# Delta-rule recurrence into a soft mixture of experts: the last step's outputs by features first, one softmax phase for the last two steps, second weights in whole rows, output columns 208 and 176, norms with fewer VectorE steps

## The chip, the cores and the metric

The kernel runs on one core of a Trainium2 chip. The metric is the device time of one execution in microseconds (us). All data are float32. Engines are named as in the profile: PE (TensorE products; PEld its weight loads), DVE (VectorE), ACT (ScalarE), POOL (GpSimd), and SP, whose queue issues most transfers.

## The reference

The first half is a delta-rule attention, the second a soft mixture of experts over its output:

```python
# q, k, v: (B, H, S, D) = (4, 8, 768, 48); beta: (B, H, S)
k_n = k / (np.linalg.norm(k, axis=-1, keepdims=True) + 1e-06)
for t in range(S):
    y[:, :, t] = q_t @ state                       # per batch and head, state is 48 x 48
    v_old = state^T k_t
    state = state + beta_t * outer(k_t, v_t - v_old)
x = y.transpose(0, 2, 1, 3).reshape(3072, 384)     # tokens x features
logits = x @ phi                                   # 32 slots = 8 experts x 4
d = softmax of logits over the tokens;  slot_input = d.T @ x
slot_out[e] = relu(slot_input[e] @ w1[e]) @ w2[e]  # w1: 384 x 1024, w2: 1024 x 384
c = softmax of logits over the slots;   out = c @ slot_out
```

(The three lines in the loop are shortened from products over all batches and heads.) Sums in the two softmaxes get 1e-9 added.

## The kernel before, in words

The sequence is cut into 12 steps n of 64 tokens, for all 32 pairs of batch and head at once; two steps make a pair g. Within a step the recurrence is solved in closed form: a Gram matrix of the keys is inverted as a triangular system, and the step's update of the state is a product with that inverse. The stages and their lines:

- **Preparing a step.** q, k and v are fetched by SP's queue (L497, L512). Keys and queries are turned (L563, copied by L574), their Gram matrices are formed (L589) and copied with masks: keys by ACT (L620, and L618 on DVE for n = 1) into a tile Gk of 16 rows of three 32-blocks, queries by L639 to L649. L675 adds two of the blocks into Gd, on POOL, for n = 1 on DVE.
- **Inverting a pair** (`invert`). DVE spreads Gd (L727); the squared norms stand on the diagonal. DVE takes a maximum with 1e-30 (L740), ACT a logarithm and an exponential (L744, L745), POOL and DVE one correction step and the weights (L750 to L759), DVE copies the weights to the diagonal of a second tile (L761) and scales (L767). Fifteen columns are solved (L777, L781). The norms are turned (L784) and put in place by POOL (L787). L799 to L818 turn the result back.
- **Joining** (`join`), for each step: small blocks are combined to 32 and 64 by products (L854, L872, L906, L917) and copies between them (L845 to L927).
- **The step** (`step`). v is scaled (L944); key products with the state (L959) are subtracted (L966); W(n) is the product with the inverse (L979, `chain[n]` in the code), copied as U (L1003); L989 adds the queries' part of the output, L1017 and L1026 update the state, L1041 the rest of the output, copied as Y by L1052. In the last step Y is formed and copied in two halves.
- **Routing and phases.** Y is turned (L1077, L1084), the logits are formed (L1102) and kept in Lt (L1108). A phase gathers the softmax over tokens for several steps with a running maximum (reduction L1150, exponential L1162, transposes L1170 and their copy L1172, slot products L1180, sums L1186). Phases cover steps (0 to 3), (4 to 7), (8 to 10), (11).
- **The rest.** L1279 turns the sums into slot inputs, copied by L1281. `first` multiplies them with the first weights (L1304, relu, transposes L1320), `second` with the second (L1339), in two parts of 192 output columns; L1348 to L1351 finish the slot outputs. `combine` forms the softmax over slots for a pair of steps (transposes L1120 and L1135, DVE L1124 to L1133, ACT L1127 and L1137), and waits for L1279. L1361 multiplies it with the slot outputs, for each group of 256 tokens and each batch; L1363 copies, L1365 stores, 24 stores in all.
- **Weights.** The first weights are 48 transfers of 256 KB (L1244); the second 32 of 384 KB (L1254), each four rows of one expert by 192 columns (runs of 768 bytes); the first 16 serve the first part of columns.

The order on each engine is not that of the code. A class `Plan` takes every operation with its engine, inputs, outputs and an assumed duration, and lists them by longest remaining path with a key; keys are moved by a table in the code (SHIFT), and some constants (SLACK, WKEEP, W2KEEP) steer how late or early work and transfers are placed. It also places buffers in one SBUF tile of 52,900 columns and in eight PSUM banks. Each engine then runs its instructions in that order. A product with no use (L480) keeps PE busy where the plan sees a hole at the start and the end.

## Time and profile before

| what | value |
|---|---|
| median of three runs | 284.46 us (282.22 to 285.74) |
| the profiled execution, its own time | 285.92 us |
| its span in the profile | 283.9 us |
| mean granted clock of TensorE | 0.984 |
| busy PE / DVE / ACT / POOL | 253.4 / 203.6 / 164.7 / 99.0 us |
| starts of W(0), W(8), W(11) | 45.66, 184.74, 227.06 us |
| first expert product (L1304) | 240.60 us |
| first, last store issued (L1365); last landing | 262.8, 280.3; 282.6 us |

Times within the profile are counted from the start of the span, and 2.0 us of the execution's own time lie outside it. A busy share is an average over stages: PE is nearly full in the last step and the expert products, and less so before. An engine's idle time matters only where a wait ends last.

### The profile page before, as it was taken

The page shows a single profiled execution, that of the slowest core. Times are in us where ns is not written, and L with a number is a line of the kernel's source. Part 1 is how long each engine was busy: PE and PEld are TensorE (multiplying, and loading weights), DVE is VectorE, ACT ScalarE, POOL GpSimd, SP SyncE. Part 2 cuts the span into 40 slices and gives each one's busy share as a digit, 9 for nine tenths or more (in the row PEclk, how much of TensorE's full clock was granted, in tenths as well). Part 3 has the DMA queues.
Part 4 walks back from the last instruction along what each step waited for, and adds up shares of the span by engine and source line. Part 5 has one row for each costly group of instructions (what it writes and reads, how often), then busy time and mean ns, then how long its engine had stood idle before and what let it go on. Part 6 is the DMA issues. An engine that isn't in the chain of part 4 may idle for free.

```text
span 283.9 us, 13766 instructions
## 1 busy us (share of the span) xinstructions
PE 253.4 (89%) x6038; PEld 211.2 (74%) x6038; DVE 203.6 (72%) x445; ACT 164.7 (58%) x350; POOL 99.0 (35%) x212
## 2 busy tenths in 40 slices
PE   8999998999987989797998998869997999999970
PEld 4777688898876978696986997768886896367860
DVE  2789988989688696789888796869971646941340
ACT  5556498678654698566778479671673452240330
POOL 8933476527730087404474027610330100000000
PEclk9999999999999999999999999989999999999995
DMA  8999982929436390066580994596997889999966
GB/s 99 142 137 145 137 90 41 135 43 139 59 50 68 68 106 3 2 82 93 99 75 2 125 236 97 163 228 218 330 373 265 246 249 322 328 301 329 289 216 223
DMA packets 105834, 45.11 MB, mean 159 GB/s; under 512 B 77008, under 2 KB 99568, under 8 KB 105776
## 3 DMA queue, kind: packets, MB, share of 16 engines
q1 hardware_dynamic: 105600, 44.05, 74.3%
q8 instruction: 47, 0.77, 1.2%
q10 hardware_dynamic: 48, 0.10, 0.3%
q0 software_dynamic: 128, 0.10, 0.2%
q14 instruction: 11, 0.09, 0.1%
HBM read 39.52 MB, written 4.72 MB: 156 GB/s over the span
## 4 chain that ended last, share of the span: by engine, by line
PE 65%; ACT 9%; DMA 7%; issue 6%; DVE 5%; SPq 3%; POOL 1%; ACTq 0%; DVEq 0%; POOLq 0%
DMA sb<-in_k_dram 7%; PE pb L589 6%; PE pb L563 6%; PE pb L989 5%; PE pb L959 5%; PE pb L979 5%; PE pb L480 4%; PE pb L872 4%; PE pb L1339 4%; PE pb L1304 4%; PE pb L1017 4%; PE pb L1041 4%; PE pb L854 3%; PE pb L917 2%; PE pb L1102 2%
## 5 line engine op out<-in xcount | busy, mean ns | idle before, releaser
L574 ACT ACTIVATE sb<-pb 128x1024 f32<-128x1024 f32 x23 | 23.5, 1025 | 17.5 <-PE pb L563 17.4
L620 ACT ACTIVATE sb<-pb,sb 128x256 f32<-128x256 f32 (+1 forms) x47 | 25.6, 574 | 7.1 <-PE pb L589 5.3
L777 DVE TENSOR_TENSOR sb<-sb 128x30 f32<-128x30 f32 (+7 forms) x90 | 27.0, 300 | 2.7
L589 PE MATMUL pb<-sb 48*64 48x64 f32 (+1 forms) x1024 | 26.3, 247 | 2.4 <-ACT sb L574 1.1
L589 PEld LDWEIGHTS pb<-sb 48*64 48x64 f32 x1024 | 22.3, 134 | 6.1 <-ACT sb L574 2.2
L563 PE MATMUL pb<-sb 128*128 128x128 f32 x192 | 25.6, 277 | 1.1 <-DMA sb<-in_k_dram 1.1
L781 DVE TENSOR_TENSOR sb<-sb 128x30 f32<-128x30 f32 (+7 forms) x90 | 23.7, 264 | 3.1
L675 POOL TENSOR_TENSOR sb<-sb 128x512 f32<-128x512 f32 x11 | 14.2, 1289 | 32.8 <-ACT sb L620 28.5
L480 PE MATMUL pb<-sb 128*128 128x512 f32 (+3 forms) x72 | 23.6, 456 | 1.1 <-DVE sb L449 1.1
L563 PEld LDWEIGHTS pb<-sb 128*128 128x128 f32 x192 | 20.9, 141 | 3.0 <-issue 1.4
L895 POOL COPY sb<-sb 32x128 f32<-32x128 f32 x48 | 13.7, 285 | 26.6 <-DVE sb L878 21.7
L1003 ACT COPY sb<-pb 64x768 f32<-64x768 f32 (+1 forms) x24 | 18.4, 765 | 6.1 <-PE pb L979 5.7
L1026 DVE TENSOR_TENSOR sb<-sb,pb 48x768 f32<-48x768 f32 x20 | 19.0, 952 | 3.7 <-PE pb L1017 3.3
L480 PEld LDWEIGHTS pb<-sb 128*128 128x128 f32 x72 | 13.0, 201 | 10.0 <-issue 7.8
L649 POOL TENSOR_SCALAR_AFFINE_SELECT sb<-sb 64x512 f32<-64x512 f32 x24 | 16.2, 676 | 11.1 <-ACT sb L645 6.9
L1041 PE MATMUL pb<-sb 128*64 128x96 f32 x384 | 18.6, 248 | 1.5 <-issue 1.5
L989 PE MATMUL pb<-sb 128*64 128x96 f32 x352 | 18.7, 260 | 0.0
L895 ACT COPY sb<-sb 32x128 f32<-32x128 f32 x48 | 14.2, 295 | 7.3 <-DVE sb L878 5.0
L1052 ACT ACTIVATE sb<-pb 128x768 f32<-128x768 f32 x11 | 8.9, 811 | 16.3 <-PE pb L1041 16.2
L1041 PEld LDWEIGHTS pb<-sb 128*64 128x64 f32 x384 | 16.6, 137 | 2.2 <-issue 1.9
L1017 PE MATMUL pb<-sb 128*48 128x96 f32 x352 | 16.9, 248 | 1.4 <-ACT sb L645 0.7
L884 DVE STREAM_TRANSPOSE sb<-sb 64x512 f32<-64x512 f32 x24 | 16.9, 705 | 0.6
(157 smaller groups left out, 544.9 us busy)
## 6 DMA issues: line engine op xcount, KB each, us to landing
sb<-in_moe_w_dram SPq DMA_DIRECT2D x48, 256.0 KB, 4.7
sb<-in_moe_w_dram SPq DMA_DIRECT2D x32, 384.0 KB, 6.6
sb<-in_k_dram SPq DMA_DIRECT2D x24, 192.0 KB, 5.5
sb<-in_v_dram SPq DMA_DIRECT2D x48, 96.0 KB, 4.4
sb<-in_q_dram SPq DMA_DIRECT2D x24, 192.0 KB, 6.1
out_dram<-sb SPq DMA_DIRECT2D x24, 192.0 KB, 2.5
sb<-in_beta_dram ACTq DMA_DIRECT2D x1, 96.0 KB, 4.9
sb<-in_moe_phi_dram POOLq DMA_DIRECT2D x2, 32.0 KB, 6.0
```

What stands on the lines that cost most here:

```text
L480: pl.filler = lambda b, w: mm(A(b)[:, 0, 0:w].rearrange("p (a f) -> p a f", f=min(w, P)), A(cone), A(cone)[:, 0:min(w, P)].unsqueeze(1).br ...
L563: nc.tensor.transpose(o[:, 128 * j:128 * j + 128], A(src)[:, 128 * j:128 * j + 128], ident())
L574: nc.scalar.activation(o, x, ACT.Copy)
L589: mm(A(ps)[ha(c ^ (j // 4)), i, w * (j - j0):w * (j - j0) + w], kq(n)[hd(i), j, c, 0:C], kq(n)[hd(i), j, c, lo:hi])
L620: nc.scalar.activation(o, i_, ACT.Copy, scale=m)
L777: V.tensor_tensor(p, blk(tt, j, j + 1, 0, m).broadcast_to(sh), blk(lb, j, j + 1, j + 1, 16).rearrange("p x a i -> p x i a").broadcast_to(s ...
L781: V.tensor_tensor(t, t, p, op=ALU.subtract)
L895: (nc.scalar.copy if by_act else nc.gpsimd.tensor_copy)(o[q:q + 32, :, c, i], zx()[64 * c + 32:64 * c + 64, y, i].rearrange("p (j t) -> p ...
L989: mm(ypart(j)[:, :, c], kq(n)[:, j, c, C:2 * C], S0()[:, j, c], start=b % 2 == 0 and c == 0)
L1017: mm(A(pS)[hd(i), j // 4, a:a + 2 * D], A(Kb[n])[:, 128 * j + 64 * i:128 * j + 64 * i + D], U0()[:, j // 4, i, j % 4])
L1026: nc.vector.tensor_tensor(o, o, x, op=ALU.add)
L1041: mm(ypart(j)[:, i], A(AT[n])[:, C * xi(i, j):C * xi(i, j) + C], U0()[:, j // 4, i, j % 4], start=n == 0 and b % 2 == 0 and i == 0)
```

## The change

- The table SHIFT, the constants SLACK, WKEEP and W2KEEP, and several assumed durations are replaced, so the order on every engine is planned anew.
- Norms: the logarithm gets 1e-30 as its bias and reads the diagonal directly, the weights are written to the second tile's diagonal by POOL, so L740 and L761 go; the layout of Gk and Gd is by j first, so L787 goes. Two reciprocals and the turning of the norms stay on DVE.
- Key copies are cut by block (in all 9 of 512 elements and 51 of 256 on ACT, instead of 22 and 25). For n = 1, 2 and 3 the sum into Gd is formed by DVE straight from PSUM (`pack`).
- Last step: the outputs are formed with features on partitions (32 + 32 products of 64 columns), the logits come from that form with a second copy of phi (cphl, four small transfers), and Y is turned back by eight transposes.
- Phases cover (0 to 3), (4 to 7), (8, 9), (10, 11); the last reads its logits from PSUM.
- `combine` no longer waits for L1279; in the new order five of six run among the steps.
- Second weights: 32 transfers of 384 KB, each two whole rows of 384 columns (3 KB runs), all used by both parts of columns; the parts are 208 and 176 columns wide.
- The output products of four batches become one operation, in which successive products use other groups of 32 rows.

```diff
-SLACK = 4.53
+SLACK = 6.8594
...
-    111: -55.2, 112: 3.5, 113: 0.7, 114: 0.6, 115: 0.2, 116: -32.3, 117: -43.4, 118: -124.6,
-    119: -58.4, 120: -98.2, 121: -59.1, 122: -57.4, 123: -156.3, 124: 3.3, 125: -131.3,
-    126: -45.2, 127: 29.5, 128: 181.8, 129: -184.9, 130: 170, 131: -144.2, 132: 56.4, 133: -23.8,
...
@@ -67,7 +70,7 @@
...
     def t_act(c):
-        return 0.17 + 0.00071 * c
+        return 0.23 + 0.0007 * c
...
     LAT, TLD = 2.3, 3.0
-    W1AT, W2AT, W2KEEP = 6, 10, 8741
+    W1AT, W2AT, W2KEEP = 6, 10, 4494.80
...
+        src2 = moe_phi.rearrange("(m i c d) s -> i c d m s", m=2, i=2, c=2)
+        for i in H2:
+            for c in H2:
+                def go2(i=i, c=c):
+                    nc.sync.dma_start(out=A(cphl)[hd(i)].rearrange("p (m c s) -> p c m s", m=2, c=2)[:, c], in_=src2[i, c])
+                pl.op("DMA", 0.3, go2, w=[(cphl, (i, c))], lat=LAT, after=after, key=50)
...
-        def ev(ys, i, lower):
+        def ev(i, b):
             def go():
...
+                x = A(ps).rearrange("p i (j f) -> p j i f", f=w)[:, :, :, 32 * (b > 0):32 * (b > 0) + 32]
+                o, m = Gb(n, b)[:, j0:j0 + nj], M1() if b == 1 else M0()
...
-                ev(H2, i, 1)
+            for b in (0, 1, 2):
+                ev(i, b)
     APART = 4
+    PACKS = (1, 2, 3)
+    def Gt(n):
+        return A(Gd[n // 2]).rearrange("p (t s j i) -> p s j i t", s=2, t=32, i=2)[:, n % 2]
+    def pack(n, j0, nj, ps, w):
+        if n in PACKS:
+            for i in H2:
+                def go(i=i):
+                    x = A(ps)[:, i].rearrange("p (j f) -> p j f", f=w)[:, :, 32:C]
+                    return nc.vector.scalar_tensor_tensor(
+                        Gt(n)[:, j0:j0 + nj, i], x, M1(), Gb(n, 0)[:, j0:j0 + nj, i], op0=ALU.mult, op1=ALU.add)
+                pl.op("DVE", t_dvp(32 * nj), go,
+                      r=[(ps, i), cm0] + [(Gk[n], (0, j0, y)) for y in (None, i)], w=[(Gd[n // 2], (n % 2, j0, i))])
...
                 ps = pl.buf(2, psum=True)
                 gram(n, 0, 2 * C, j0, 4, ps)
                 keys(n, j0, 4, ps, 2 * C)
+                pack(n, j0, 4, ps, 2 * C)
                 queries(n, j0, 4, ps, 2 * C)
-        def pack():
...
-        pl.op("DVE" if n == 1 else "POOL", 0.90 if n == 1 else 1.35, pack, r=[Gk[n]], w=[(Gd[n // 2], n % 2)], port=True)
+        if n not in PACKS:
+            pl.op("POOL", 1.35, lambda: nc.gpsimd.tensor_tensor(Gt(n), Gb(n, 0), Gb(n, 1), op=ALU.add),
+                  r=[(Gk[n], (x, 0, None)) for x in H2] + [(Gk[n], (x, 4, None)) for x in H2], w=[(Gd[n // 2], n % 2)], port=True)
         return og if n < 2 else None
     def prep_q(n):
...
-        ssq, nrm, rn, gm = [pl.buf(32 * G) for _ in range(4)]
+        nrm, rn, gm = [pl.buf(32 * G) for _ in range(3)]
...
-        pl.op("DVE", W_, lambda: V.tensor_scalar(sv(ssq), sv(ssq0) if head else dg(lb), 1e-30, None, op0=ALU.max),
-              r=[ssq0 if head else lb], w=[ssq], key=-25 if head else 0)
+        ssq = ssq0 if head else lb
+        sq = lambda: sv(ssq0) if head else dg(lb)
         def root():
-            nc.scalar.activation(A(nrm), A(ssq), ACT.Ln)
+            nc.scalar.activation(sv(nrm), sq(), ACT.Ln, bias=A(cm0)[:, 7:8])
             nc.scalar.activation(A(nrm), A(nrm), ACT.Exp, scale=0.5)
-        pl.op("ACT", 0.44, root, r=[ssq], w=[nrm])
...
         def norm():
-            G_.tensor_tensor(A(rn), A(rn), A(ssq), op=ALU.mult)
+            G_.tensor_tensor(sv(rn), sv(rn), sq(), op=ALU.mult)
...
-            G_.tensor_tensor(A(gm), A(gm), A(cbb)[:, 32 * gs[0]:32 * gs[0] + 32 * G], op=ALU.mult)
+            G_.tensor_tensor(dg(tt), sv(gm), sv2(cbb), op=ALU.mult)
...
-        pl.op("POOL", 0.57, weight, r=[rn, (cbb, min(gs[0], 1))], w=[gm], port=True)
-        pl.op("DVE", W_, lambda: V.tensor_copy(dg(tt), sv(gm)), r=[gm], w=[tt])
+        pl.op("POOL", 0.57, weight, r=[rn, (cbb, min(gs[0], 1))], w=[gm, tt], port=True)
...
-        nTc = pl.buf(32 * G)
-        pl.op("DVE", 0.14, lambda: V.transpose(A(nTc), A(nrm)), r=[nrm], w=[nTc])
-        def place():
-            nc.gpsimd.tensor_copy(A(nT).rearrange("p (s j i) -> p s i j", s=4 * G, i=2),
-                                  A(nTc).rearrange("p (s i j) -> p s i j", s=4 * G, i=2))
-        pl.op("POOL", 0.2, place, r=[nTc], w=[nT], port=True)
+        pl.op("DVE", 0.14, lambda: V.transpose(A(nT), A(nrm)), r=[nrm], w=[nT])
...
-            pl.op("PE", **t_pe(16, 0.085, 96.0), fn=qs, r=[(KQ[n], 1), (KQ[n], 3), cS], w=[pY],
-                        after=[chain[n]])
-        U0 = lambda: A(cU).rearrange("p (y i j f) -> p y i j f", y=2, i=2, j=4)
...
+            def qst():
+                for j in range(8):
+                    for c in H2:
+                        for i in H2:
+                            a = D * (2 * (2 * j + c) + i)
+                            mm(A(pY)[ha(i), c, C * j:C * j + C], A(cS)[hd(i), a:a + C], kq(n)[hd(i), j, c, C:2 * C],
+                               start=j == 0)
+            if last:
+                pl.op("PE", **t_pe(32, 0.04, 24.0), fn=qst, r=[(KQ[n], 1), (KQ[n], 3), cS], w=[pY])
+            else:
+                pl.op("PE", **t_pe(16, 0.085, 96.0), fn=qs, r=[(KQ[n], 1), (KQ[n], 3), cS], w=[pY],
+                      after=[chain[n]])
...
-        parts = [(None, range(B))] if n < N - 1 else [(o, range(2 * o, 2 * o + 2)) for o in H2]
         Y = Yb[n] = pl.buf(16 * D)
-        for o, bs in parts:
-            def au(bs=bs):
-                for b in bs:
+        if last:
...
+            def aut():
+                for j in range(8):
                     for i in H2:
-                        for j in (2 * b, 2 * b + 1):
-                            mm(ypart(j)[:, i], A(AT[n])[:, C * xi(i, j):C * xi(i, j) + C],
-                               U0()[:, j // 4, i, j % 4],
...
-            oau[n] = pl.op("PE", **t_pe(4 * len(bs), 0.079, 96.0), fn=au,
-                           r=[(b, (y, c)) for b in (AT[n], cU) for y in (H2 if o is None else (o,)) for c in H2],
-                           w=[(pY, o)])
...
...
+                        for c in H2:
+                            a = D * (2 * (8 * (j // 4) + 4 * i + j % 4) + c)
+                            mm(A(pY)[ha(i), c, C * j:C * j + C], A(cU)[ha(c), a:a + C],
+                               A(AT[n])[ha(c), C * xi(i, j):C * xi(i, j) + C], start=False)
+            pl.op("PE", **t_pe(32, 0.0275, 24.0), fn=aut, r=[AT[n], cU], w=[pY])
+            for c in H2:
+                pl.op("DVE" if c else "ACT", t_dvp(512) if c else t_act(512) - 0.03, lambda c=c: (
+                    nc.vector.tensor_copy if c else nc.scalar.copy)(A(YT)[:, 512 * c:512 * c + 512], A(pY)[:, c]),
+                    r=[(pY, c)], w=[(YT, c)])
+            ps = pl.buf(2, psum=True)
+            for o in H2:
+                def back(o=o):
+                    for b in (0, 1):
+                        for c in H2:
+                            x = A(ps)[:, o, 256 * b:256 * b + 256].rearrange("p (i c f) -> p c i f", i=2, c=2)[:, c]
+                            a = 512 * c + 128 * (2 * o + b)
+                            nc.tensor.transpose(x, A(YT)[:, a:a + 128], ident())
+                pl.op("PE", **t_tr(4), fn=back, r=[YT, cident], w=[(ps, o)], key=5)
+                def yev(o=o):
...
+            return
...
-            pl.op("PE", **t_tr(len(qs6)), fn=yt, r=[(Y, o), cident], w=[(ps, o)])
...
-        pL = pl.buf(1, psum=True)
-        w = C * ns
-        parts = [(None, range(B))] if n < N - 1 else [(o, range(2 * o, 2 * o + 2)) for o in H2]
-        for o_, bs in parts:
-            def lg(bs=bs):
...
-            pl.op("PE", **t_pe(4 * len(bs), 0.0297 * ns, 32.0 * ns), fn=lg,
-                  r=[(YT, None if o_ is None else 2 + o_), cphi], w=[(pL, o_)])
...
+        pL = pLb[n] = pLb[n - 1] if n == N - 1 else pl.buf(1, psum=True)
+        w, z0 = C * ns, C if n == N - 1 else 0
+        def lg():
+            if n == N - 1:
+                for c in H2:
+                    for m in H2:
+                        for b in range(B):
+                            a = 32 * (2 * m + c)
+                            mm(A(pL)[32 * b:32 * b + 32, 0, z0:z0 + C], A(cphl)[:, a:a + 32],
+                               A(YT)[:, 512 * c + C * (2 * b + m):512 * c + C * (2 * b + m) + C], start=m == 0 and c == 0)
+                return
...
+        if n == N - 2:
...
-        pl.op("ACT", t_act(w), lev, r=[pL], w=[(Lt, n - x) for x in range(ns)])
+        pl.op("ACT", t_act(w), lev, r=[pL], w=[(Lt, n), (Lt, n - 1)])
...
-        lr = [(Lt, n) for n in range(n0, n1)]
+        late = n1 == N
+        lr = [pLb[n0]] if late else [(Lt, n) for n in range(n0, n1)]
+        lx = lambda: A(pLb[n0])[:, 0, 0:C * nn] if late else A(Lt)[:, C * n0:C * n1]
...
-    PH = [(0, 4), (4, 8), (8, 11), (11, 12)]
-    LEAD, VLEAD, WKEEP = 5, 3, 4836
...
@@ -1243,17 +1288,15 @@
...
-    HD = Dm // 2
-    for hc in H2:
+    HDS = (208, Dm - 208)
+    for tp in range(NFC // 2):
         for e in range(E):
-            for t4 in H2:
-                w2b[e, t4, hc] = t = pl.buf(4 * HD)
-                def go(e=e, t4=t4, hc=hc, t=t):
-                    s = moe_w2[e].rearrange("(p t) d -> p t d", t=NFC)
-                    nc.sync.dma_start(out=A(t).rearrange("p (t d) -> p t d", t=4),
-                                      in_=s[:, 4 * t4:4 * t4 + 4, HD * hc:HD * hc + HD])
-                pl.op("DMA", 1.17, go, w=[t], lat=LAT, after=[chain[W2AT]], key=200 + 100 * hc + 0.1 * e, keep=W2KEEP)
+            w2b[e, tp] = t = pl.buf(2 * Dm)
+            def go(e=e, tp=tp, t=t):
+                s = moe_w2[e].rearrange("(p t) d -> p t d", t=NFC)
+                nc.sync.dma_start(out=A(t).rearrange("p (t d) -> p t d", t=2), in_=s[:, 2 * tp:2 * tp + 2])
+            pl.op("DMA", 1.06, go, w=[t], lat=LAT, after=[chain[W2AT]], key=200 + 10 * (e // 4) + tp, keep=W2KEEP)
...
-        combine(g, [ot3])
+        combine(g, [])
...
-        cols = slice(HD * hc, HD * hc + HD)
+        HD = HDS[hc]
+        cols = slice(HDS[0] * hc, HDS[0] * hc + HD)
...
-                           A(w2b[4 * qq + j, tp // 2, hc])[:, HD * (t % 4):HD * (t % 4) + HD], start=qq == 0 and t == 0)
-            return pl.op("PE", 0.66, ni=32, ut=768.0, fn=prod, r=[(hTb[qq], tp // 2)] + [w2b[4 * qq + j, tp // 2, hc] for j in range(4)],
+                           A(w2b[4 * qq + j, tp])[:, Dm * (t % 2) + HDS[0] * hc:Dm * (t % 2) + HDS[0] * hc + HD], start=qq == 0 and t == 0)
...
+            po = [pl.buf(1, psum=True) for _ in range(B)]
+            def prod(po=po, so=so, T0=T0, HD=HD):
+                for par in H2:
+                    for b in range(B):
+                        rg = slice(32 * b, 32 * b + 32)
+                        mm(A(po[b])[:, 0, HD * par:HD * par + HD], A(cT)[rg, T0 + par:T0 + 256:2], A(so)[rg])
...
-                po, ob = pl.buf(1, psum=True), pl.buf(2 * HD)
-                def prod(po=po, so=so, T0=T0, b=b):
-                    rg = slice(32 * b, 32 * b + 32)
-                    for par in H2:
-                        mm(A(po)[:, 0, HD * par:HD * par + HD], A(cT)[rg, T0 + par:T0 + 256:2], A(so)[rg])
-                pl.op("PE", 0.28, prod, r=[cT, so], w=[po], ni=8, ut=200.0)
```

209 lines of the change are left out of this document (101 added, 108 removed), and 44 rows, old and new, of the table SHIFT.

## The prediction

> **What bounds the kernel now.** I read the page first, for the share of each engine and the chain that ended last, then that chain in the last quarter, windows over the stages, the waits around the worst stage, and rows for what the change touches. All times are us.
>
> ```profile
> PE 253.4 (89%) x6038; PEld 211.2 (74%) x6038; DVE 203.6 (72%) x445; ACT 164.7 (58%) x350; POOL 99.0 (35%) x212
> PE 65%; ACT 9%; DMA 7%; issue 6%; DVE 5%; SPq 3%; POOL 1%; ACTq 0%; DVEq 0%; POOLq 0%
> ```
>
> TensorE is the bound, but only 65% of the chain is its work: the rest are hand-overs between engines.
>
> ```profile
> 45.60:227.10 181.50, 162.11 (x4498) 145.11 (x4490) 145.51 (x296) 120.63 (x234) 69.90 (x147) 0.99 0.64 131
> 186.00:189.40 3.40, 1.51 (x38) 1.34 (x37) 1.60 (x7) 2.17 (x3) 0.00 (x0) 1.00 1.11 149
> 189.40:192.80 3.40, 3.40 (x62) 2.98 (x66) 3.03 (x7) 1.90 (x5) 1.14 (x4) 0.50 0.96 305
> PE pb L1170 <- ACT sb L1003: 2.0, 1, 2.0
> ```
>
> Each window gives its length, then busy time of PE, PEld, DVE, ACT, POOL, the granted clock, the DMA share and GB/s. The first runs from step 0's product with the inverse, W(0) (L979), to step 11's, W(11): of 181.5, PE is busy 162.1, idle 19.4. The next two are one stage in it: four transposes of the second softmax phase (L1170) stand in PE's order behind W(8) and wait 2.0, with them all that follows; then the clock is granted at 0.50 for a window.
>
> The chain of waits after W(11), pieces as start, length, what:
>
> ```profile
> 227.06 1.15 PE pb L979 x64
> ...
> 233.89 0.36 PE pb L480 x2
> 234.25 0.35 PE pb L1170 x3
> ...
> 240.05 0.55 PE pb L1120 x3
> 240.60 10.48 PE pb L1304 x96
> 251.08 2.09 PE pb L1320 x16
> 253.17 0.83 PE pb L1135 x6
> 254.00 6.01 PE pb L1339 x144
> ...
> 261.32 4.46 PE pb L1361 x47
> 265.78 4.08 PE pb L1339 x96
> ...
> 271.41 0.93 PE pb L1361 x8
> ```
>
> So there are three stages: recurrence to 227.06, last step and phases 13.5 up to the expert products (L1304), and from there 42.05 to the last landing at 282.62. (A product stands as two records: L1339's 144 are 72 products, 0.083 each; L1361's 47 are 24, 0.186 each.)
>
> **The change, part by part.** The sum stands against the profiled run, 285.92 (span 283.9); the median of the three is 284.46, 1.46 less, and the same difference is applied to it.
>
> *Head.* The new order puts the spreading of the first inverse about 1.1 earlier on VectorE, but four new packs (0.45 each, estimated from the 256-element row of L620, 0.476), a scaling of v (L944, 1.06) and the second pair's spread (L727, 1.22) ahead of step 0's correction. Bounds −1 and +1.5 (these rows less the 1.1 and what waits on PE anyway); I take **+0.5**.
>
> *TensorE work ahead of W(11).* Adding the rows by the new order gives 187.7 before W(11) instead of 184.0: ten combine transposes (L1120, L1135; 0.27 to 0.14 each, about 1.5) come from behind the first expert products, the phase over steps 8 and 9 (two transposes, the slot products of two steps) lies here (about 1.15 by L1170's and L1180's rows), and the last step's 32 query products stand ahead of its key products (about 1.3, from L989's 1.47 for 32 records); smaller moves take 0.3 off. **+3.7**. Part of it fills holes: the two phase transposes and single combine transposes stand behind W(n), where PE waits for ACT's copy of U (L1003, 0.79 for each half). Between 0 and 3.7 is hidden; I take **−1.5**, because PE idles 19.4 in this span, but 7.3 of that is "issue", which no filling removes.
>
> *The second phase's stall.* In the new order its four transposes stand behind the state products (L1017), so nothing waits in front of them. The 2.0 goes. So does the cold window, if the stall made it: L989 took 2.62 in it instead of 1.47, L1180 1.77 instead of 1.46, 1.5 together. Late next is L1003 itself, as in every other step, which is already in the sum. **−3.5** (bounds −2.0 and −3.5).
>
> *Norms.* The change says "without VectorE", but two reciprocals and a transpose stay; what goes is a maximum and a copy on VectorE and a POOL copy.
>
> ```profile
> L740 DVE TENSOR_SCALAR sb<-sb 128x32 f32<-128x32 f32 x6 | 4.3, 712 | 0.3
> L761 DVE COPY sb<-sb 128x32 f32<-128x32 f32 x6 | 1.7, 284 | 0.0
> ```
>
> Six inversions, five beyond the head: 5 × (0.712 + 0.284) = 5.0 of VectorE time. The chain shows L740 only in 174.4–184.7 (0.55), where VectorE and POOL alone lead to W(8). So one pair counts, **−1.0** (bounds 0 and −5.0).
>
> *Keys on ACT.* The new split is 9 operations of 512 and 51 of 256 elements, not 22 and 25. By the rows (0.686, 0.476) that is 30.4 instead of 27.0: +3.4 of ACT. ACT is busy 120.6 of 181.5, so I take 0; what covers it is that idle third, and without cover it is +3.4. The packs that leave POOL (L675, 1.29 each) for VectorE are costed in the head.
>
> *From W(11) to the expert products.* Now 13.5. By rows: W 1.15, U copies to 2.34, 32 feature-first products 1.3 (as L989) minus overlap to 3.75, copy 0.7, logits 0.65, reduction and minimum 0.45, exponential 0.7 (to 7.0), transposes 0.35, their copy behind another ACT step to 8.15, products 0.85, sacc update 0.6, L1279 1.17, copy 0.27: 11.4. The second phase's round (L1170 to L1180, 234.25–237.62) and the transposes ahead of the logits (L1077, about 1.0) are what is missing from it; eight new transposes back run beside the exponential. **−2.1** (bounds −0.5, if ACT's steps queue as in keys; −3).
>
> *Combines and tail.* L1120 (0.55) is inside the last sum; L1135's 0.83 leaves the chain. Six combines (DVE rows sum to 1.49, ACT 0.59 each) lay beside L1304, where POOL is idle (0.00 in 240.6–254.0); five now lie in the steps, VectorE at 145.5 of 181.5: cost 0, with the cover gone +7.5 (a rival). Output columns 208 + 176 leave the second products' sum unchanged (208 + 176 = 2 × 192) and make part 1's 24 output products longer by 208/192. These now rotate over four row groups instead of two in a row on one; their price lies between 0.186 and L1339's 0.083, and I take 0.14, the middle, since no row shows rotation with this shape: 24 × 0.14 × 1.083 = 3.64, not 4.46. Part 2's twelve issues of 192 KB tiles become 176 wide:
>
> ```profile
> L1365 SPq DMA_DIRECT2D out_dram<-sb x24: 533/582/1032, 262.8 to 280.3; - x24
> DMA to landing us min/median/max: 2.3/2.5/4.0
> ```
>
> An issue takes SP about 0.58 whatever its width, so the end follows the first one. **−1.6** (0.83 + 0.8; bounds −0.5 at 0.186, −3.1 at 0.083).
>
> [...]
>
> *Weights.* 48 first-weight tiles go at 0.67 per 256 KB; the second weights now at rows of 3 KB, no longer 768 B, with all 32 tiles due in part 1 (before: half of them).
>
> ```profile
> sb<-in_moe_w_dram SPq DMA_DIRECT2D x48, 256.0 KB, 4.7
> sb<-in_moe_w_dram SPq DMA_DIRECT2D x32, 384.0 KB, 6.6
> ```
>
> The 32 issues run from 219.58 and land to 265.76, 1.18 apart when nothing blocks. In the new placement the eleventh tile's space is freed by step 11's subtraction (L966), right ahead of W(11). At 1.18 the last lands 22 × 1.18 + 2.7 (the shortest landing of L1244) = 28.7 after W(11). The last eighth of the second products of part 1 needs it at 11.4 + 10.48 + 2.09 + 7/8 × 64 × 0.083 × 208/192 = 29.0. At 1.0 apart (0.67 × 384/256, the longer runs) 4 are to spare. I take **0** (bounds 0 and +3).
>
> Sum: 0.5 + 3.7 − 1.5 − 3.5 − 1.0 − 2.1 − 1.6 = −5.5. Profiled 280.4, median **279.0**.
>
> **Rivals.** The 2% that a measurement of this kernel can tell from no change is 5.7: below 278.8 faster, above 290.1 slower.
>
> *Faster: norms and holes count in full.* If every inversion's chain shortens as 174–184.7 suggests, 4.0 more goes: 275.0; if the 3.7 is hidden wholly, 272.8. For: L740 runs from 0.19 to 1.39, always in front of ACT's logarithm. Against: the chain shows it once.
>
> [...]
>
> *ACT the new bound.* Keys +3.4 and five combines' ACT 2.9 on the path: 285.3, slower than 284.46 though within 2%. For: ACT alone leads in 99.0–106.7 and 138.2–144.6. Against: two thirds busy.
>
> *Second weights late.* At 1.18 the margin is 0.3, and the last tiles reuse space that first expert products hold until late; three of them queued behind such a wait at 1.18 give about +3, 282. Against: the first weights' rate.
>
> *Combines blocked by POOL, slower.* Five combines bring 25 VectorE operations that read SBUF only beside POOL's work. If each loses what L740 loses (0.712 − 0.190 = 0.52), that is 13.1 on the chain of VectorE: 292. It turns the sign once 5.5 of it is on the path and leaves the 2% at 11.1. For: L740's and L761's spread (188 to 684 ns), while L1130 beside no POOL spreads only 274 to 288. Against: VectorE is idle 36 of 181.5, and combines have slack.
>
> [...]
>
> **How the numbers follow.** Forecast 279.0, own range 276.5 to 281.5, chance 0.46, of which 0.20 lies below 278.8; full norms 0.24; packing 0.05; ACT 0.10; weights 0.09; blocked combines 0.06. Faster 0.20 + 0.24 + 0.05 = 0.49; slower 0.06; within 2% the remaining 0.45. The range 273.5 to 285.0 leaves out the blocked combines, about half of ACT's case and a third of the full-norm case: 0.2.
>
> **What would show it.** No PE wait at the second phase's transposes and clock 1.0 around W(8) (3.5); W(11) about 1.8 earlier than 227.06 (0.5 + 3.7 − 1.5 − 3.5 − 1.0); the first expert product 11.4 after it; no wait of L1383 (the second products) for weights; part 1's output products under 0.15 each; Ln right behind the spread. Wrong if W(11) comes later than 227, if short VectorE operations of the combines average above 0.6, or if ACT becomes the engine that PE waits for most.

## The result, and the profile after

The changed kernel takes 295.88 us (median of four; three of them 294.09 to 296.40), the kernel before beside it 284.48 (282.22 to 285.74): a ratio of 1.0389, 95% interval 1.0293 to 1.0485. It is slower by 11.4, where 5.5 less was forecast. The execution first profiled ran at a granted clock of 0.56 from end to end (397.66), so every reading of "after" is from a second profiled execution of the same kernel, 297.06 with a span of 295.2, against the 285.92 and 283.9 of before.

The page of after: busy time of each engine, and the chain that ended last by engine.

```profile
PE 257.2 (87%) x6100; PEld 212.8 (72%) x6100; DVE 200.3 (68%) x439; ACT 167.0 (57%) x362; POOL 97.5 (33%) x205
...
PE 40%; DVE 22%; ACT 12%; issue 7%; DMA 6%; SPq 4%; POOL 4%; ACTq 0%; DVEq 0%; POOLq 0%
```

TensorE is busy 3.8 longer, but it has lost much of the chain (40%, was 65%), and VectorE has gained (22%, was 5%). Windows over the stages of after, with columns as before:

```profile
32.81:36.22 3.41, 1.68 (x38) 1.31 (x34) 3.41 (x7) 2.16 (x5) 2.14 (x5) 1.00 1.50 146
36.22:39.63 3.41, 3.41 (x40) 3.05 (x38) 2.93 (x4) 2.11 (x4) 0.94 (x3) 0.50 1.04 148
51.24:236.77 185.53, 166.68 (x4622) 148.36 (x4622) 149.59 (x316) 125.03 (x263) 71.21 (x142) 0.99 0.60 133
189.50:202.86 13.36, 11.29 (x334) 9.66 (x330) 12.57 (x33) 7.21 (x15) 1.15 (x4) 1.00 0.89 289
...
221.10:223.50 2.40, 0.00 (x0) 0.00 (x1) 1.40 (x6) 1.42 (x7) 0.00 (x0) 1.00 1.00 368
242.40:244.40 2.00, 0.05 (x2) 0.00 (x0) 0.00 (x0) 0.00 (x0) 0.00 (x0) 1.00 1.00 396
```

The first two are the head, the stage ahead of W(0): a window in which PE works 1.68 of 3.41, then one at half clock (a cold window, below), and three more behind it. The third runs from W(0) to W(11): 185.5, not 181.5. The fourth is W(8) to W(9), at full clock and without the old wait: 13.4 instead of 15.9. In the last two PE stands still for nearly all of 2.4 and 2.0, with the DMA share at 1.00. PE's waits in after from W(8) to the first expert product (waited in total, times, longest):

```profile
PE pb L992 <- issue: 2.4, 1, 2.4
PE pb L1133 <- issue: 2.0, 1, 2.0
PE pb L1002 <- issue: 1.1, 1, 1.1
...
PE pb L1215 <- ACT sb L923: 0.5, 1, 0.5
```

"issue" is a wait for nothing that the profile shows. The phase's transposes (now L1215) wait 0.5. The chain of waits after W(11):

```profile
236.77 1.15 PE pb L992 x64
...
241.88 0.57 PE pb L1133 x28
242.45 1.98 issue
244.43 0.43 PE pb L1133 x4
...
252.06 7.86 PE pb L1347 x72
...
272.83 0.92 PE pb L1405 x16
```

L1133, the last step's logits, is cut in two by one of those waits, behind 28 of its 32 records. An output operation (L1405) holds eight products and takes 0.92, 0.115 each, where 0.14 was assumed and 0.186 was measured before. But the stores:

```profile
L1411 SPq DMA_DIRECT2D out_dram<-sb x24: 569/582/2030, 274.3 to 291.8; - x24
...
DMA to landing us min/median/max: 2.3/2.5/4.5
```

The first is issued 22.3 after the first expert product and the last 17.5 later, just as before (22.2 and 17.5). Not for the same reason: before, the thirteenth store is issued 2.25 behind the twelfth, held by the second part's outputs; in after the last output product ends 3.4 earlier (32.0 behind the first expert product, not 35.4), but two of SP's issues take 1.12 and 2.03 (the longest in the line) instead of 0.58.

The stages, in us from the first record of each, for this pair of profiles, and for a pair in which both kernels fetch only an eighth of each expert weight tile (`before_light` and `light` below, called the light pair):

| stage | before | after | difference | before, light | after, light | difference |
|---|---|---|---|---|---|---|
| start to W(0) | 45.5 | 51.2 | +5.8 | 45.2 | 51.9 | +6.6 |
| W(0) to W(8) | 139.3 | 138.3 | −1.0 | 136.0 | 137.7 | +1.7 |
| W(8) to W(9) | 15.9 | 13.4 | −2.6 | 13.9 | 13.4 | −0.6 |
| W(9) to W(10) | 14.7 | 17.8 | +3.1 | 13.4 | 17.8 | +4.4 |
| W(10) to W(11) | 11.7 | 16.1 | +4.4 | 10.6 | 12.4 | +1.7 |
| W(11) to first expert product | 13.5 | 15.2 | +1.7 | 13.3 | 11.4 | −1.9 |
| from there to the end | 43.3 | 43.2 | −0.1 | 43.3 | 42.5 | −0.8 |
| span | 283.9 | 295.2 | +11.3 | 275.8 | 286.8 | +11.1 |

### The profile page after: what moved, and what is told of

Read it like the earlier page. It is cut to its first block, busy times and chain, and to the rows that moved or that the text cites. A ratio compares the mean times of both kernels' runs of the same rounds, so it can differ in the third digit from the quotient of the medians.

```text
span 396.0 us, 13891 instructions
## 1 busy us (share of the span) xinstructions
PE 383.7 (97%) x6100; PEld 294.1 (74%) x6100; DVE 201.5 (51%) x439; ACT 170.5 (43%) x362; POOL 95.6 (24%) x205
## 3 DMA queue, kind: packets, MB, share of 16 engines
q1 hardware_dynamic: 93760, 44.10, 51.2%
## 4 chain that ended last, share of the span: by engine, by line
PE 96%; DVE 1%; issue 0%; DVEq 0%; ACT 0%
PE pb L575 10%; PE pb L601 9%; PE pb L484 8%; PE pb L972 7%; PE pb L1039 6%; PE pb L1093 6%; PE pb L1002 6%; PE pb L886 5%; PE pb L1383 5%; PE pb L1347 5%; PE pb L868 5%; PE pb L992 5%; PE pb L1115 3%; PE pb L930 3%; PE pb L920 3%; PE pb L1142 2%
## 5 line engine op out<-in xcount | busy, mean ns | idle before, releaser
L601 PE MATMUL pb<-sb 48*64 48x64 f32 (+1 forms) x1024 | 41.0, 326 | 1.1 <-ACT sb L586 1.1
L575 PE MATMUL pb<-sb 128*128 128x128 f32 x192 | 40.8, 387 | 0.0
L601 PEld LDWEIGHTS pb<-sb 48*64 48x64 f32 x1024 | 31.3, 171 | 8.4 <-issue 2.4
L575 PEld LDWEIGHTS pb<-sb 128*128 128x128 f32 x192 | 29.3, 172 | 8.3 <-issue 3.1
L484 PE MATMUL pb<-sb 128*128 128x512 f32 (+3 forms) x68 | 33.1, 638 | 1.2 <-DVE sb L452 1.1
L972 PE MATMUL pb<-sb 128*64 128x96 f32 x352 | 27.5, 340 | 0.0
L1093 PE MATMUL pb<-sb 128*64 128x96 f32 x352 | 27.2, 340 | 0.0
L1039 PE MATMUL pb<-sb 128*48 128x96 f32 x352 | 26.7, 336 | 0.0
L484 PEld LDWEIGHTS pb<-sb 128*128 128x128 f32 x68 | 15.8, 254 | 13.8 <-issue 11.2
L1093 PEld LDWEIGHTS pb<-sb 128*64 128x64 f32 x352 | 23.6, 172 | 3.0 <-issue 1.6
L972 PEld LDWEIGHTS pb<-sb 128*64 128x64 f32 x352 | 23.4, 175 | 2.9 <-issue 0.6
L1039 PEld LDWEIGHTS pb<-sb 128*48 128x48 f32 x352 | 21.6, 152 | 4.3 <-issue 2.3
L1002 PE MATMUL pb<-sb 128*64 128x96 f32 x320 | 24.2, 334 | 0.0
L909 POOL COPY sb<-sb 32x128 f32<-32x128 f32 x48 | 15.2, 317 | 34.9 <-PE pb L930 20.6
L860 POOL COPY sb<-sb 64x256 f32<-64x256 f32 x12 | 7.3, 610 | 63.9 <-DVE sb L815 59.2
```

Of the source, the lines that this page charges most:

```text
L484: pl.filler = lambda b, w: mm(A(b)[:, 0, 0:w].rearrange("p (a f) -> p a f", f=min(w, P)), A(cone), A(cone)[:, 0:min(w, P)].unsqueeze(1).br ...
L575: nc.tensor.transpose(o[:, 128 * j:128 * j + 128], A(src)[:, 128 * j:128 * j + 128], ident())
L601: mm(A(ps)[ha(c ^ (j // 4)), i, w * (j - j0):w * (j - j0) + w], kq(n)[hd(i), j, c, 0:C], kq(n)[hd(i), j, c, lo:hi])
L972: mm(A(pR)[ha(c ^ (j // 4)), j // 4, 2 * D * (j % 4):2 * D * (j % 4) + 2 * D], kq(n)[:, j, c, 0:C], S0()[:, j, c])
L1002: mm(ypart(j)[:, :, c], kq(n)[:, j, c, C:2 * C], S0()[:, j, c], start=b % 2 == 0 and c == 0)
L1039: mm(A(pS)[hd(i), j // 4, a:a + 2 * D], A(Kb[n])[:, 128 * j + 64 * i:128 * j + 64 * i + D], U0()[:, j // 4, i, j % 4])
```

## The experiments

Each "before" is the median of the kernel before, measured beside the run. Runs without an interval are single profiled executions. A ratio is to that before; its 95% interval stands in brackets.

**The kernel again** (`after_again`, no edit), to tell a slow clock from a slow order.

> The changed kernel once more, for a profile at the full clock (the first one ran at a granted clock of 0.56 all through). Theory A (clock): the extra 10.4 us over the kernel before lie mostly in windows at clock 0.50: the mean granted clock of its other runs, 0.948 to 0.960 against 0.984, means some 26 us of such windows instead of 9 (share at half clock = 2 x (1 - clock)), worth about 8 us; so the profile should show five or more such windows ahead of W(11), and W(11) late by about 10. Theory B (order): the clock differs little where the time is lost; instead waits on ACT or VectorE grow by 10 us ahead of W(11). Theory C (weights): the second products wait for their weights in the tail, up to 10 us, and the low clock is a result of that wait.

Measured: 297.06, mean clock 0.949. Theory C falls: no wait of the second products (L1383) for weights is in the profile. The signs of A came, five cold windows ahead of W(11) and W(11) 9.7 late, but four of the five lie in the head, and W(9) to W(10) is late without one. The table has both.

**The head.** PE's hole (idle time) at 33 to 35 is a wait of the fillers (L484) for VectorE, which forms the new packs (L650) from PSUM (PE's waits in after, 25 to 52):

```profile
PE pb L484 <- DVE sb L650: 1.7, 1, 1.7
```

`packs_pool` gives those of n = 2 and 3 back to POOL; `head_fill` adds to that edit six fillers of 512 columns ahead of the first joining product.

```diff
+                    if n > 1:
+                        return nc.gpsimd.tensor_tensor(Gt(n)[:, j0:j0 + nj, i], Gb(n, 0)[:, j0:j0 + nj, i],
+                                                       Gb(n, 1)[:, j0:j0 + nj, i], op=ALU.add)
...
+            if o.fn.__code__.co_name == "m16" if hasattr(o.fn, "__code__") else False:
+                if not done:
+                    for _ in range(6):
+                        self.filler(bank, 512)
+                done = True
             o.fn()
```

> The changed kernel in its own order, but the packs of steps 2 and 3 are formed by POOL from the copied tile, as before the change, not by VectorE from PSUM (four additions of 256 elements instead of four VectorE operations). In the changed kernel the filler product at 32.84 us waits 1.73 us for those packs, PE is busy 1.68 of 3.41 in the clock window 32.81 to 36.22, and the next four windows, to 49.87, run at clock 0.50; W(0) starts at 51.24 against 45.48. Theory A (packs hold PSUM banks, PE idles, the clock halves): the wait goes, no half clock ahead of W(0), W(0) at 46 to 47, total 4 to 5 us less than the changed kernel (about 290 to 291). Theory B (the head is late for another reason, scale_v waiting for v's transfer ahead of the inverse on VectorE): W(0) stays within 1 us of 51.

> The kernel of packs_pool with six more filler products of 512 columns ahead of the first join product (L868), where PE otherwise waits for ACT and POOL between 33 and 36 us; nothing else. The profiles so far give W(0) at 48.68, 50.28, 51.24, 52.99 and 53.22 with 1, 3, 4, 5 and 5 windows at half clock ahead of it, about 1.1 us each. Theory A (the head is late because PE idles there and then runs at half clock): no half clock between 20 and 50 us, W(0) at 46.5 to 48, total near 289 to 290 and the runs closer together. Theory B (half clock comes from elsewhere, or the fillers delay the join): half-clock windows stay, W(0) at 49 or later.

Measured: `packs_pool` 293.65, ratio 1.0232 (1.0138 to 1.0326), where the first joining product now waits 3.4 for POOL; `head_fill` 289.70, ratio 1.0189 (1.0028 to 1.0350), with no cold window in the head. Its W(0) is still at 49.0: the six fillers run to 38.6 and the first joining product stands behind them on PE, while POOL's packs are done at 37.0 (in `packs_pool` that product starts at 37.2). Over the profiles of after (the one of 297.06) and of its variants, the hole, the cold windows that follow it in the head and the start of W(0); in the last four the head itself was edited:

| run | hole, us | windows at 0.50 | W(0) |
|---|---|---|---|
| light_nocomb | 0.85 | 0 | 45.4 |
| copy_act | 2.27 | 1 | 46.9 |
| two_queues | 2.31 | 3 | 50.3 |
| after_again | 1.73 | 4 | 51.2 |
| light | 2.29 | 4 | 51.9 |
| light_early | 2.28 | 4 | 51.9 |
| shift64 | 2.29 | 5 | 53.2 |
| packs_pool | 3.38 | 1 | 48.7 |
| packs_queues | 2.75 | 5 | 53.0 |
| light_norms | 4.20 | 4 | 54.0 |
| head_fill | none | 0 | 49.0 |

The kernel before has no such hole: W(0) is at 45.5 in before, and at 45.2 in `before_light`. The five rows with a hole of 2.3 and the head's work unchanged have 1 to 5 cold windows, and W(0) moves by 1.57 for each ((53.2 − 46.9)/4); carried on to none, that gives 45.4, as before. So by this estimate the order costs next to nothing here by itself, and the clock costs about 1.6 for each window. `light_nocomb`, without a cold window, is at 45.4 too, but its hole is shorter. How many windows there are differs between executions with the same hole.

**What PE waits for when nothing shows.** `shift64` replaces the first four fillers by twenty of 128 columns, 64 more instructions on PE, and changes nothing else.

```diff
+            if o.seq == -1 and left:
+                left -= 1
+                for _ in range(5):
+                    self.filler(next(iter(o.bufs)), 128)
```

> The changed kernel, with the first four filler products of 512 columns replaced by twenty of 128, 64 more PE instructions ahead of all else; the work and its order stay. It moves only the places where PE's code is fetched (16 KB pieces, one for each 256 PE instructions). Theory A (code fetches fall badly in the changed kernel: 2.40 us in the middle of W(10) and 1.98 in the last logits, each followed by a window at half clock): the stalls at these two places go or shrink below 1.5, W(8) to the first expert product shortens by 2 to 5 us (from 62.5), others may appear. Theory B (the stalls come with the weight transfers, wherever the fetch falls): stalls of 2 us or more stand elsewhere between W(8) and the expert products, and that stretch stays within 1 us.

Measured: 295.97, ratio 1.0331 (1.0229 to 1.0434); the stalls are now 2.09 at 205.09, 1.90 at 221.5 and 1.91 at 241.9, that is, in front of other instructions, and no shorter: theory B, though the stretch from W(8) to the expert products is 1.3 shorter. In after the queue of instructions (q8) moves 48 packets of 16 KB (0.79 MB) for PE's 12,200 instructions, one for about 254. One of them lies in 221.0 to 222.2 and one in 242.0 to 243.2, where PE stalls for 2.4 and 2.0. The second of these windows:

```profile
q1 hardware_dynamic: 171, 0.46, 97.4%
q8 instruction: 1, 0.02, 5.4%
```

(242.0 to 243.2; packets, MB, share of 16 engines.) PE stops at 242.45 and goes on at 244.43. `light` and `before_light` fetch an eighth of the columns of every expert weight tile, so their expert products run on other data.

```diff
-                nc.sync.dma_start(out=A(t)[:, 512 * x:512 * x + 512], in_=s[:, kk, 512 * x:512 * x + 512])
+                nc.sync.dma_start(out=A(t)[:, 512 * x:512 * x + 64], in_=s[:, kk, 512 * x:512 * x + 64])
```

> The changed kernel, in which each transfer of expert weights moves an eighth of its columns (so the expert products use what else lies in the buffers); same instructions and order. Theory A (a code fetch waits behind the weights' packets): the stalls for code between W(8) and the first expert product, 5.5 to 5.9 us in sum in the profiles so far, against 2.1 in the kernel before, fall below 3, and that stretch from 61 to 63 to about 58 to 59. Theory B (they come from where the fetches fall in a denser stream of PE instructions): the sum stays above 4.5.

> The kernel before, in which each transfer of expert weights moves an eighth of its columns (the expert products use what else lies in the buffers); instructions and order as before. It is the pair to light, where the stretch W(8) to the first expert product fell from 61-63 to 54.86 us with no stall for code above 0.3. Theory A (the change makes that stretch no shorter by itself, what differs is stalls for code): the stalls of the kernel before, 2.1 in sum in that stretch of 55.83, go as well and it comes to 53 to 54.5, level with light or shorter. Theory B (the change shortens the work and only the stalls hide it): the stretch stays at 55.5 or more.

Measured: `light` 288.54, `before_light` 277.60. From W(8) to the first expert product no unexplained stall of over 0.4 is left in either, so the stalls there come with the weight traffic (DMA share 1.00 in both of after's). That they are fetches of PE's code which queue behind it is a reading of the packets, not shown by itself. (Ahead of W(8), `light` still has one of 1.3.) But the table shows that the kernel before paid as much: with less of it its span is 8.1 shorter, that of after 8.4. Before pays more of it ahead of W(8) (139.3 to 136.0), after more behind it, where its three stalls of over one us stop PE for 5.5 in sum (1.1 + 2.4 + 2.0) and those of before for 3.4 (2.0 + 1.4). The difference between the kernels is nearly the same without the traffic and with it, 11.1 and 11.3. The stalls explain where after loses time, not that it loses.

One of those of before had been read wrongly. The 2.0 of L1170 behind W(8) in before is preceded by such a packet (before, 185.3 to 186.4):

```profile
q8 instruction: 1, 0.02, 5.3%
```

It starts at 185.41, and PE goes on at 187.89. And in `before_light` the same transposes run straight behind W(8) (PE), while ACT's L1003 is still copying:

```profile
181.18 1.15 PE L979 MATMUL pb<-sb 64*64 64x48 f32 x64 [0.47 <-DVE sb L927]
182.33 0.60 PE L1170 MATMUL pb<-sb 128*128 128x128 f32 x4
...
182.40 1.61 ACT L1003 COPY sb<-pb 64x768 f32<-64x768 f32 x2
```

`before_phase` moves only these transposes, behind the queries' products.

```diff
         order = self.schedule()
+        order.insert(863, order.pop(855))
```

> The kernel before with one move in TensorE's order: the four transposes of the second softmax phase (L1170), which stand right behind W(8) and wait 2.0 with everything behind them, are put behind the queries' products (L989, L990 here). Nothing else is touched, so pair 5's columns on VectorE stay where they are. Theory A (the stall was on the path for good, as the forecast's -3.5 has it): W(8) to W(9) falls from 15.9 to 12.5-13.5, W(9) to W(10) stays near 14.7, and the time falls by 2.0 to 3.5, ratio 0.988 to 0.993. Theory B (the gain is given back one step later, because W(10) hangs on pair 5's columns on VectorE and on the copies behind them, not on W(9)): W(8) to W(9) falls as much, W(9) to W(10) grows to 16.5 or more, and the time moves by less than 1.5, ratio 0.995 to 1.005.

Measured: 285.24 against 284.86, ratio 1.0026 (0.9986 to 1.0066). Both theories took for granted that the wait would go. It did not:

```profile
PE pb L873 <- ACT sb L1004: 2.2, 1, 2.2
```

L873 is the joining product (L872 of before) that now stands behind W(8). The transposes waited 2.0 there and it waits 2.2, from 183.56 to 185.78, which the profile puts down to ACT's last copy. That ACT does not end the wait is seen in `before_best` (below), which has the same order there: L873 starts while ACT's copies still run, to 184.93.

```profile
184.70 1.07 PE L873 MATMUL pb<-sb 128*64 128x32 f32 x31 [1.47 <-ACT sb L1004]
...
183.32 1.61 ACT L1004 COPY sb<-pb 64x768 f32<-64x768 f32 x2
```

So the stall never belonged to the phase.

**W(9) to W(10), 17.8 instead of 13.4 without any stall.** In after pair 5's columns on VectorE end 2.5 behind the start of W(9), in before 0.3: VectorE, in order, has the combine's steps, the last joining copy of step 8 (L940), step 9's join (L892, L898) and the phase's maximum ahead of the scaling (L789). Then come POOL's copies (after):

```profile
208.41 1.70 POOL L834 COPY sb<-sb 32x256 f32<-32x256 f32 x4 [0.52 <-DVE sb L823]
210.17 2.62 POOL L860 COPY sb<-sb 64x256 f32<-64x256 f32 x1
...
210.72 1.81 DVE L956 TENSOR_TENSOR sb<-sb 128x768 f32<-128x768 f32 x2
```

The copy takes 2.62 instead of 0.39, and ends 0.3 behind VectorE's two operations with two inputs from SBUF. `copy_act` gives that copy to ACT.

```diff
-            (nc.scalar.copy if e == "ACT" else nc.gpsimd.tensor_copy)(
+            (nc.scalar.copy if e == "ACT" or n == N - 1 else nc.gpsimd.tensor_copy)(
```

> The changed kernel with one POOL copy of step 11's join (64 x 256, the last of L860) made by ACT; nothing else. In four of five profiles that copy took 2.61 to 2.71 us instead of 0.39 and stood in the chain of waits between W(9) and W(10), while VectorE ran two multiplications with two SBUF inputs (L956). Theory A (POOL is shut out by VectorE): the first product behind it (L868, second time after W(9)) starts about 2 us sooner, at W(9) + 7.8 instead of 10.0, and W(9) to W(10) shortens by 1 to 2 from 17.8, unless a code fetch takes it. Theory B (the next wait, VectorE's or ACT's, ends at the same time): W(9) to W(10) stays above 17.3.

Measured: 291.56, ratio 1.0183 (1.0019 to 1.0346), its profile with one cold window in the head. W(9) to W(10) is 17.9, and the joining product behind the copy still starts 10.1 after W(9). But this profile has a stall without a cause shown of 1.4 in that stage, from 199.8, and from there to the joining product PE idles 0.24 only: the run doesn't tell what the copy costs. In `light`, without a stall, PE waits 0.46 for it. Three more, all on `light`, one execution each: `light_nocomb` leaves out five combines, `light_norms` puts the maximum and the copy of the norms back on VectorE, `light_early` moves pair 5's scaling and first five columns right behind L940.

```diff
+            V.tensor_scalar(sq(), sq(), 1e-30, None, op0=ALU.max)
             nc.scalar.activation(sv(nrm), sq(), ACT.Ln, bias=A(cm0)[:, 7:8])
...
-            G_.tensor_tensor(dg(tt), sv(gm), sv2(cbb), op=ALU.mult)
+            G_.tensor_tensor(sv(gm), sv(gm), sv2(cbb), op=ALU.mult)
+            V.tensor_copy(dg(tt), sv(gm))
...
+        gone = {id(o) for a in kinds.values() for o in a[:5]}
...
+            if id(o) not in gone:
+                o.fn()
...
+        early = [order[i] for i in (870, 872, 874, 877, 882, 884)]
+        at = order[852]
...
+            if o is at:
+                for p in early:
+                    p.fn()
```

The first part is `light_norms`; `kinds` holds the operations of `combine` by kind, and the last part is `light_early`.

> light without the five combines that the change moved into the steps (their transposes, VectorE and ACT operations are left out, the table they fill is zero); all else in the same order. With an eighth of the weights no code stall disturbs the reading: W(0) to the first expert product was 192.51 in light, W(8) to W(11) 43.49. Theory A (the combines cost on the path, as the forecast's rival had it, 5 x 1.49 of VectorE and more): W(0) to the first expert product shortens by 4 to 8. Theory B (they lie in holes, as the forecast's 0 had it): by less than 1.5. If ACT's chain between W(9) and W(10) is what they lengthen, that interval alone falls from 17.77 by about 0.6 to 1.2.

> light with the two VectorE steps of the norms put back (the maximum with 1e-30 ahead of the logarithm, and the copy of the weights to the diagonal), in each of six inversions, in the same order. Theory A (one pair on the path, the forecast): W(0) to the first expert product 1.0 longer than 192.51. Theory B (every inversion's chain): 4 to 5 longer. Theory C (nothing, other work on VectorE stands ahead of the scaling anyway): within 0.5.

> light with the scaling and the first five columns of pair 5 (L789, L799, L803) put on VectorE right behind W(8)'s correction, where the kernel before has them, ahead of the join of step 9. In light, pair 5's columns end 2.5 after W(9), in the kernel before 0.3. Theory A (the late columns make W(9) to W(10) long): W(9) to W(10) falls from 17.77 by 1.5 to 2.5, and W(8) to W(9) grows by less than 1. Theory B (ACT's and POOL's copies set it): W(9) to W(10) stays above 17.

| run | time | W(0) | W(0) to first expert product | W(9) to W(10) |
|---|---|---|---|---|
| light | 288.54 | 51.9 | 192.5 | 17.8 |
| light_nocomb | 282.08 | 45.4 | 193.0 | 17.8 |
| light_norms | 293.48 | 54.0 | 194.6 | 17.8 |
| light_early | 293.31 | 51.9 | 197.2 | 17.8 |

The 6.5 that `light_nocomb` is faster lie in the head, where no cold window fell; behind W(0) it gains nothing (about 0.9, if the 1.4 that W(5) to W(6) is longer around its one cold window at 134 is taken off). So the combines are nearly free. Without them POOL has long copies all the same, the ones just ahead, of which four take 3.88 instead of 1.70 (`light_nocomb`, W(9) to W(10)):

```profile
202.79 3.88 POOL L843 COPY sb<-sb 32x256 f32<-32x256 f32 x4 [0.48 <-DVE sb L832]
```

The norms count: back on VectorE they cost 2.1 behind W(0), and 2.2 before it, where their hole grows from 2.29 to 4.20. `light_early` missed its aim. The columns moved up, but step 9's join, which they passed, was late:

```profile
POOL sb L915 <- DVE sb L898: 5.3, 1, 5.3
...
PE pb L926 <- ACT sb L1031: 3.8, 1, 3.8
```

W(8) to W(9) grew from 13.4 to 18.4, with two cold windows behind that wait, and the last column still ended 2.5 behind W(9). It only shows that VectorE has no room there: of the two, the one that comes second is late for what follows. Most of the longer stage is PE's own work. The stage in `light` and in `before_light`:

```profile
202.87:220.64 17.77, 16.08 (x460) 14.03 (x460) 15.51 (x31) 11.71 (x29) 6.51 (x13) 1.00 0.30 60
195.09:208.48 13.39, 12.77 (x391) 11.80 (x391) 11.02 (x14) 9.29 (x20) 4.75 (x10) 1.00 0.21 46
```

Of the 4.4, 3.3 is work that the new order puts here, and 1.1 idle time of PE. Yet `light_nocomb` took 1.2 of this work away (14.9 busy) and the stage did not shrink, so the chain of hand-overs with the other engines must be about as long as PE's work.

**The tail.** `two_queues` issues the stores of batches 1 and 3 from ACT's queue; `packs_queues` adds the edit of `packs_pool`.

```diff
-                pl.op("DMA", 0.125 + 0.00267 * HD, lambda ob=ob, b=b, T0=T0, cols=cols: nc.sync.dma_start(
+                pl.op("DMA", 0.125 + 0.00267 * HD, lambda ob=ob, b=b, T0=T0, cols=cols: (nc.scalar if b % 2 else nc.sync).dma_start(
```

> The changed kernel, with the stores of batches 1 and 3 issued from ACT's queue instead of SP's; nothing else. In the changed kernel all 24 stores leave SP in a row, 0.675 us apart, from 274.3 to 291.8, though the last output product ends at 284.0. Theory A (the tail is SP's issuing): the stores end about 2.9 us after the last copy, near 288, total 5 us less (about 290.5). Theory B (the transfers themselves or the copies bound the tail): total within 1 us of the changed kernel.

> Both edits together: packs of steps 2 and 3 by POOL, and stores of batches 1 and 3 from ACT's queue. If head and tail are independent, the gains add: about 9 to 10 us less than the changed kernel, 285 to 287, so level with the kernel before. If the head's gain is absorbed by the next wait (weights, code), less than 7.

Measured: `two_queues` 291.99, ratio 1.0123 (1.0023 to 1.0223), the stretch from the first expert product to the end 41.3 instead of 43.2; `packs_queues` 292.19, ratio 1.0198 (1.0111 to 1.0286), with five cold windows in the head of its profile, so the two gains did not add. Then the rotation alone, in the kernel before at 192 + 192 columns (`before_rot`), the same with the stores of batch 3 from ACT's queue (`before_rot_q`), and that with the move of `before_phase` (`before_best`).

```diff
-                    for par in H2:
-                        mm(A(po)[:, 0, HD * par:HD * par + HD], A(cT)[rg, T0 + par:T0 + 256:2], A(so)[rg])
+            for par in H2:
+                for b in range(B):
+                    rg = slice(32 * b, 32 * b + 32)
+                    mm(A(po[b])[:, 0, HD * par:HD * par + HD], A(cT)[rg, T0 + par:T0 + 256:2], A(so)[rg])
...
-                pl.op("DMA", 0.6, lambda ob=ob, b=b, T0=T0, cols=cols: nc.sync.dma_start(
+                pl.op("DMA", 0.6, lambda ob=ob, b=b, T0=T0, cols=cols: (nc.scalar if b == 3 else nc.sync).dma_start(
```

> The kernel before with part 8 of the change alone, columns still 192 and 192: the output products of four batches as one operation that rotates over the row groups. All ahead of the tail keeps its order. Theory A (the products get shorter, 0.115 each as in the changed kernel instead of 0.186, but the end follows the first store by 24 issues of 0.675 and 2.3): the last landing moves from 282.6 by 1.4 at most, total 0.5 to 1.5 us less. Theory B (the end follows PE): 24 x 0.07 = 1.7 or more less.

> before_rot, with the stores of batch 3 issued from ACT's queue (6 of 24). Theory A (SP's issuing bounds the tail): part 2's nine stores on SP end at about 271.2 + 8 x 0.675 + 2.9 = 279.5, 3 us ahead of the kernel before, total 2 to 3.5 us less than it. Theory B (copies or landing bound): within 1 us of before_rot.

> before_rot_q (the output products rotated over four row groups, the stores of batch 3 from ACT's queue) with the same move of the phase's transposes. Theory A: both gains add, ratio 0.980 to 0.985. Theory B: no better than before_rot_q alone, 0.987 to 0.995. In both the last stretch, from the first expert product to the end, stays near 41.2.

Measured: `before_rot` 282.92 against 283.94, ratio 0.9999 (0.9955 to 1.0042): no difference shown in the time. In its profile the last stretch is 41.7 instead of 43.3, and 43.3 it is in all three profiles with the old tail. `before_rot_q` 281.69, ratio 0.9910 (0.9872 to 0.9948), about 0.9% faster than before, the last stretch 41.2. `before_best` 282.67 against 284.86, ratio 0.9931 (0.9886 to 0.9976): the phase's move adds nothing. The stores of `before_rot`, and of `before_rot_q` on two queues:

```profile
L1367 SPq DMA_DIRECT2D out_dram<-sb x24: 534/582/877, 261.6 to 277.5; - x24
...
L1367 SPq DMA_DIRECT2D out_dram<-sb x18: 534/586/1062, 258.4 to 272.9; - x18
...
L1367 ACTq DMA_DIRECT2D out_dram<-sb x6: 541/542/632, 260.3 to 272.0; - x6
```

From the first to the last is 17.5 in before, 16.0 with the rotation, and 14.5 with the second queue. The first step is the products: the second part's first store comes 30.7 after the first expert product instead of 32.4, and the eleven behind it follow at 0.67 as before. The second step saves 1.5 of issuing but only 0.5 of the end, because the last landing then takes 3.8 from its issue instead of 2.3.

## Why the prediction was wrong, step by step

- **Head, +0.5.** This step failed: it priced the added VectorE work at its own length and put the clock at nothing. As an order it was right (45.4 without cold windows, against 45.5). That VectorE's packs leave PE a hole, and that the half clock behind it puts W(0) 1.4 to 7.7 later, was not looked for. In the pair of profiles it is +5.8, half of the loss.
- **The second phase's stall, −3.5.** The largest gain in the sum, and the reading behind it was false: the line "L1170 <- ACT sb L1003: 2.0" was taken for a wait for ACT, which does not end it (`before_light`, `before_best`); a packet of code starts in front of it, at 185.41. What the change itself gains in W(8) to W(9) is 0.6, by the light pair. In the first pair the stage did get 2.6 shorter, by luck: no such stall fell into it. "Late next" was the next such stall, two of which (2.4 and 2.0) fell between W(10) and the first expert product.
- **TensorE work ahead of W(11), +3.7, hidden −1.5.** Too low and not hidden. In the light pair PE is busy 164.8 instead of 159.5 from W(0) to W(11), 5.3 more: the ten combine transposes are 2.8 where 1.5 was put, the last step's queries 2.0 where 1.3 was put. PE's idle time there did not shrink to hide them but grew, from 14.4 to 16.3. So the stretch from W(0) to W(11), which the forecast had 2.3 shorter (3.7 − 1.5 − 3.5 − 1.0), is 7.2 longer in the light pair: 5.3 of work and 1.9 of idle time.
- **Where this work lies.** 3.3 of the 5.3 stand between W(9) and W(10) and 1.7 between W(10) and W(11), which is all that the latter stage grows by in the light pair. W(9) to W(10) grows by 1.1 more. There the order puts the scaling of pair 5 behind 4.1 of other VectorE work, and the columns end 2.5 instead of 0.3 behind W(9); POOL's copy takes 2.2 longer (2.62 instead of 0.39), of which PE sees 0.46. The forecast has no step for either. Which hand-over would have to be shorter for the stage to shrink stays open: `light_early` moved another wait in, `copy_act` was disturbed by a stall of 1.4, and in `light_nocomb` the long copies of POOL came one step earlier.
- **Norms, −1.0.** Too small where it could be tested: 2.1 behind W(0), in a single execution, inside the bounds of 0 and 5.0, and 2.2 in the head, which the step left out. In the last pair, on which the step was sized, nothing came of it: the scaling comes 8.4 after the spread's end instead of 5.8. The rival "norms count in full" was right in part, yet the time went up.
- **From W(11) to the expert products, −2.1, to 11.4.** Right in size: 11.4 and −1.9 in the light pair; with the stall of 2.0, 15.2. In part this is luck: the pieces listed add up to 6.25 where the text has 7.0, and from its 8.15 to 11.04, so about 1.1 of the 11.4 stands for no row.
- **Tail, −1.6.** Not seen in the time, and −0.1 in the pair of profiles, though the product fell under the assumed price (0.115 against 0.14). Its mechanism holds as far as the products go: with the rotation alone the last stretch of the kernel before is 1.6 shorter, because the end follows the second part's first store; and the median issue stayed at 0.582, with 208 and 176 columns as with 192. What it left out is that in the new kernel SP's own issues bind, and some of them take longer: with the stores of two batches on ACT's queue the last stretch is 41.3 (`two_queues`), and the 1.9 more in after is nearly what its two long issues (1.12 and 2.03) take beyond 0.58 each, 2.0 in sum. What makes them long is not shown. No run shows output products of 0.083, the price behind a tail of −3.1 (the chance of 0.05 for packing): they took 0.115, a factor of 1.6 below 0.186, and the end did not follow them.
- **Combines 0, weights 0, keys on ACT 0.** Held. The combines' VectorE operations keep their lengths (L1172: 0.272 mean), so the rival that POOL blocks them fell; what took longer was POOL's own copy, 2.62 instead of 0.39. Between W(0) and the first expert product PE's waits put down to ACT sum to 5.2 instead of 8.6, of which 2.0 was the misread stall, so ACT did not become the bound. The combines' 0 is shown by `light_nocomb`; the keys' 0 was not tested by itself.
- **Signs named beforehand.** W(11) at 236.8, later than 227, says wrong, and the first expert product comes 15.2 after it, not 11.4. A wait of only 0.5 at the phase's transposes and clock 1.0 around W(8) came true for another reason than the one given, and so proved nothing. Output products of 0.115, no wait of L1383 for weights and a logarithm 0.04 to 1.1 behind the spread (0.6 to 2.6 before) came true, and none of them moved the end.

The sum of the differences in the light pair: head +6.6, W(0) to the first expert product +5.3, tail −0.8, together 11.1 of span.
